# The order of r's weight tiles behind attention: tiles for both batches first

## The chip, the cores and the metric

The kernel runs on one core of one Trainium2 chip. The metric is device time of one execution in microseconds (us); lower is better. A core has a matrix engine (TensorE, PE in the rows, with its weight loads as PEld), VectorE (DVE), ScalarE (ACT), GpSimd (POOL) and SyncE (SP), which here issues the transfers (DMA) from memory.

## The reference

For two batches, causal attention over 12 heads (448 tokens, 64 channels a head) gives x (448 x 768 a batch). A token and channel mixer follows, then a gated block. Cut to its formulas:

```python
scores = np.where(mask, -1e9, q @ k.T / 8); attn = softmax(scores)
x = attn @ v                                  # (2, 448, 768)
h = np.maximum(x.T @ w_tok1, 0) @ w_tok2      # mixes tokens
u = x + h.T
r = np.maximum(u @ w_ch1, 0)                  # 768 -> 1536 channels
y = u + r @ w_ch2                             # 1536 -> 768 channels
uv = gelu(y @ w_in); a, b = halves of uv
out = y + (a * (w_sg @ layernorm(b) * g + b_sg)) @ w_out
```

The large weights come as float64 and are used with about float32 accuracy.

## The kernel before, in words

**Numbers.** Every operand of the large products is held as a pair of tiles, a high and a low part, and `mm3` (L132) makes three matmuls of each product: high by high, low by high, high by low.

**Weight tiles.** A weight tile of 128 x 768 numbers goes through one path (`load64`, L96, through `load_w`, L124). SyncE loads the raw float64 words (`wraw`, 768 KB, two buffers). ScalarE turns their upper halves into float32 (`wm`, L113, three buffers), VectorE shifts `wm` (L116) and adds bits of the lower halves (L117), ScalarE rounds `wm` to the high part (`whi`, L121, three buffers), and GpSimd subtracts it from `wm` for the low part (`wlo`, L94, three buffers). TensorE reads `whi` in a group's first matmul and `wlo` in its second or third.

**Stages.** Attention and the token mixer (L196 to L443) make u, batch 0 first and then batch 1, as `u_hi` and `u_lo`. Beside the second batch's attention, seven of the twelve tiles of r are made for batch 0 (`up`, L411; `NF0` is 7). Behind attention comes the **r stage** (L456): `channel_up` (L170) loads a tile of `w_ch1`, and for each batch that it is asked for makes a group of 18 matmuls (6 chunks by 3) into `r_ps`, and from it `rh` (ScalarE, L179) and `rl` (VectorE, L180). Tiles 0 to 6 are asked for batch 1 alone there, one group each, and tiles 7 to 11 for both batches, two groups each: 17 groups in all. Then the **y stage** (L458): for each of 6 output chunks, `channel_down` (L183) loads two halves of `w_ch2`, 768 KB each, and makes a group of 36 matmuls a batch, whose first 18 read the first half and the rest the second, in order of r's tiles; beside it a 512 KB tile of `w_in` is prepared as `wvh` and `wvl` (L460). The gated block follows.

**Order.** Each engine runs its instructions in the order in which a scheduler lists them; the scheduler goes by the program's order and a timeline of its own. An engine waits at an instruction until its operands and its output buffer are ready, and all behind it on that engine waits too.

Of the kernel before, what the change touches and what calls it, by code (L numbers as in the profile page):

```python
# [27 lines left out]
def mixer_kernel(  # L28
# [27 lines left out]
    NFF = 12  # L56
# [3 lines left out]
    NF0 = 7  # L60
# [35 lines left out]
    def load64(hi, lo, src, hi_eng="act", twice=False):  # L96


        n = src.shape[-1]
        raw = wpool.tile([P, WC], mybir.dt.int64, tag="wraw", name="wraw", bufs=2)[:, :n]  # L100
        if twice:
            nc.sync.dma_start(raw[:64], src)
            nc.sync.dma_start(raw[64:], src)
        else:
            nc.sync.dma_start(raw, src)
        words = raw.bitcast(I32).rearrange("p (n w) -> p n w", w=2)
        m = wpool.tile([P, WC], F32, tag="wm", name="wm", bufs=3)[:, :n]
        mi = m.bitcast(I32)

        nc.scalar.activation(  # L113
            m, words.bitcast(F32)[:, :, 1], AF.Prelu, scale=2.0 ** -112, alpha=-(2.0 ** 32)
        )
        nc.vector.tensor_scalar(mi, mi, 3, None, ALU.logical_shift_left)  # L116
        nc.vector.scalar_tensor_tensor(mi, words[:, :, 0], 29, mi, ALU.logical_shift_right, ALU.bitwise_or)  # L117
        if hi_eng == "pool":
            nc.gpsimd.tensor_scalar(hi, m, 1.0, 0.0, ALU.mult, ALU.add)
        else:  # L120
            nc.scalar.copy(hi, m)  # L121
        sub(lo, m, hi)
# [47 lines left out]
    def channel_up(m, batches, pool, psum):  # L170

        wh, wl = load_w(w_ch1[m])
        for b in batches:
            us = slice(b * S, (b + 1) * S)
            pr = psum.tile([P, 512], F32, tag="d", name="r_ps")
            mm3(pr[:, :S], [((wh[:, c, :], wl[:, c, :]), (u_hi[:, c, us], u_lo[:, c, us])) for c in range(NCC)])
            rh = pool.tile([P, S], F32R, tag=f"rh{m}_{b}", name="rh")
            rl = pool.tile([P, S], F32R, tag=f"rl{m}_{b}", name="rl")
            nc.scalar.activation(rh, pr[:, :S], AF.Relu)  # L179
            nc.vector.scalar_tensor_tensor(rl, pr[:, :S], 0.0, f32(rh), ALU.max, ALU.subtract)  # L180
            r_of[m, b] = (rh, rl)

    def channel_down(m, psum, tmp):  # L183

        ws = [load_w(w_ch2[m, :, c:c + NCC, :]) for c in (0, NCC)]
        for b in range(B):
            us = slice(b * S, (b + 1) * S)
            py = psum.tile([P, 512], F32, tag="d", name="y_ps")
            mm3(py[:, :S], [((ws[c // NCC][0][:, c % NCC, :], ws[c // NCC][1][:, c % NCC, :]), r_of[c, b]) for c in range(NFF)])
            t = tmp.tile([P, S], F32, tag="yt", name="yt")  # L190
            nc.vector.tensor_add(t, py[:, :S], f32(u_hi[:, m, us]))
            nc.vector.tensor_add(t, t, f32(u_lo[:, m, us]))
            nc.scalar.copy(u_hi[:, m, us], t)  # L193
            sub(u_lo[:, m, us], t, u_hi[:, m, us])
# [257 lines left out]
    with rs:  # L452
        ps_d = ctx.enter_context(tc.tile_pool(name="ps_d", bufs=8, space=PSUM, reuse_waits="tile"))
        r1pool = rs.enter_context(tc.tile_pool(name="r1pool", bufs=1, reuse_waits="tile"))
        tmp = rs.enter_context(tc.tile_pool(name="tmp", bufs=3, reuse_waits="tile"))
        for m in range(NFF):  # L456
            channel_up(m, [1] if m < NF0 else [0, 1], r1pool, ps_d)
        for m in range(NCC):  # L458
            channel_down(m, ps_d, tmp)
            load64(wvh[:, m, :], wvl[:, m, :], w_inv[:, m, :])  # L460
# [158 lines left out]
```

## Time and profile before

| | |
|---|---|
| time, median of 3 runs (lowest, highest) | 428.57 us (427.43, 428.97) |
| profiled execution: its own time | 429.13 us |
| profiled execution: its span, first to last instruction | 427.3 us |
| TensorE busy | 399.9 us, 94% of the span |
| mean granted TensorE clock, as a share of full speed | 0.988 |
| r stage (first group to first matmul of the y stage) | 169.02 to 231.12 us of the span |

The profiled execution is one run, 0.56 us above the median; 1.83 us of its time lie outside the span. Times in rows count from the span's start. Matmuls are pipelined, so one row lasts longer than the step from it to the next; the steps between starts tell TensorE's pace.

### The profile page before, as it was taken

The page shows a single profiled execution, that of the slowest core. Times are in us where ns is not written, and L with a number is a line of the kernel's source. Part 1 is how long each engine was busy: PE and PEld are TensorE (multiplying, and loading weights), DVE is VectorE, ACT ScalarE, POOL GpSimd, SP SyncE. Part 2 cuts the span into 40 slices and gives each one's busy share as a digit, 9 for nine tenths or more (in the row PEclk, how much of TensorE's full clock was granted, in tenths as well). Part 3 has the DMA queues.
Part 4 walks back from the last instruction along what each step waited for, and adds up shares of the span by engine and source line. Part 5 has one row for each costly group of instructions (what it writes and reads, how often), then busy time and mean ns, then how long its engine had stood idle before and what let it go on. Part 6 is the DMA issues. An engine that isn't in the chain of part 4 may idle for free.

```text
span 427.3 us, 6998 instructions
## 1 busy us (share of the span) xinstructions
PE 399.9 (94%) x2567; PEld 340.3 (80%) x2567; DVE 238.4 (56%) x522; ACT 204.2 (48%) x389; POOL 246.5 (58%) x234
## 2 busy tenths in 40 slices
PE   5878788888998999999999999999999999999996
PEld 3545666776787998999999999999998889965995
DVE  5989566787693645344444275557437451249422
ACT  3888678697665454445344244334423232332100
POOL 2789768769777564464335247454556653225662
PEclk9989999999898999999999999999999999999999
DMA  7999999999987854446344344453354001100122
GB/s 213 199 290 235 209 173 208 252 220 265 242 170 164 163 160 154 137 156 220 123 132 157 106 127 144 134 181 110 126 163 135 0 0 51 49 2 0 76 98 86
DMA packets 66738, 62.29 MB, mean 146 GB/s; under 512 B 53136, under 2 KB 58384, under 8 KB 66704
## 3 DMA queue, kind: packets, MB, share of 16 engines
q1 hardware_dynamic: 66704, 61.85, 56.5%
q8 instruction: 20, 0.33, 0.3%
q14 instruction: 14, 0.11, 0.1%
HBM read 46.50 MB, written 2.75 MB: 115 GB/s over the span
## 4 chain that ended last, share of the span: by engine, by line
PE 67%; DMA 12%; POOL 8%; ACT 5%; SPq 2%; issue 2%; DVE 2%; POOLq 0%; ACTq 0%; DVEq 0%
DMA pT<-hl 8%; PE y_ps L137 7%; PE y_ps L136 7%; PE y_ps L138 7%; PE r_ps L138 6%; PE r_ps L136 6%; PE r_ps L137 6%; POOL hl L301 4%; DMA vr<-in 2%; PE v_ps L138 2%; PE o_ps L136 2%; PE o_ps L138 2%; PE o_ps L137 2%; PE ug_ps L136 2%; PE v_ps L137 2%; PE ug_ps L138 2%
## 5 line engine op out<-in xcount | busy, mean ns | idle before, releaser
L94 POOL TENSOR_TENSOR wlo<-wm,whi 128x768 fp32r<-128x768 f32 (+1 forms) x41 | 81.3, 1984 | 75.6 <-ACT whi L121 75.1
L116 DVE TENSOR_SCALAR wm<-wm 128x768 int32<-128x768 int32 (+2 forms) x53 | 34.1, 643 | 88.0 <-ACT wm L113 88.0
L301 POOL TENSOR_TENSOR hl<-pe,hl 128x512 f16<-128x512 f32 x48 | 60.5, 1267 | 29.2 <-ACT hl L300 25.2
L113 ACT ACTIVATE wm<-wraw 128x768 f32<-128x768 f32 (+2 forms) x53 | 42.7, 805 | 59.1 <-POOL wlo L94 47.7
L286 PE MATMUL s_ps<-k,q 128*128 128x64 f32 (+3 forms) x216 | 57.9, 410 | 8.3 <-DMA q<-in 4.6
L138 PE MATMUL r_ps<-u_hi,wlo 128*128 128x448 f32 x144 | 53.4, 370 | 0.0
L137 PE MATMUL r_ps<-u_lo,whi 128*128 128x448 f32 x144 | 53.2, 369 | 0.0
L136 PE MATMUL r_ps<-u_hi,whi 128*128 128x448 f32 x144 | 53.1, 369 | 0.0
L136 PE MATMUL y_ps<-rh,whi 128*128 128x448 f32 x144 | 52.6, 365 | 0.0
L138 PE MATMUL y_ps<-rh,wlo 128*128 128x448 f32 x144 | 52.6, 365 | 0.0
L137 PE MATMUL y_ps<-rl,whi 128*128 128x448 f32 x144 | 52.6, 365 | 0.0
L121 ACT CAST whi<-wm 128x768 fp32r<-128x768 f32 (+1 forms) x41 | 32.8, 800 | 37.8 <-PE ug_ps L137 11.6
L117 DVE SCALAR_TENSOR_TENSOR wm<-wraw,wm 128x768 int32<-128x768 int32 (+2 forms) x53 | 50.1, 945 | 1.0
L286 PEld LDWEIGHTS s_ps<-k,q 128*128 128x128 f32 x216 | 32.4, 208 | 17.2 <-issue 6.6
L298 ACT ACTIVATE pe<-pe,bias 128x192 f32<-128x192 f32 (+3 forms) x84 | 40.2, 522 | 0.4
L291 DVE CUSTOM_DVE_ANT_0 pe<-s_ps,mask 128x320 f32<-128x320 f32 (+3 forms) x84 | 34.6, 444 | 7.9 <-PE s_ps L286 6.1
L300 ACT CAST hl<-pe 128x512 f16<-128x512 f32 x48 | 29.3, 612 | 18.3 <-DMA pT<-hl 17.9
L326 PE MATMUL x_ps<-vh,pT 128*128 128x65 f16 (+1 forms) x240 | 26.3, 197 | 11.6 <-DMA pT<-hl 10.9
L326 PEld LDWEIGHTS <-pT 128*128 128x128 f16 (+1 forms) x240 | 21.2, 98 | 19.6 <-DMA pT<-hl 14.6
L94 POOL TENSOR_TENSOR u_lo<-yt,u_hi 128x448 fp32r<-128x448 f32 x12 | 13.9, 1156 | 30.1 <-ACT u_hi L193 30.1
L138 PEld LDWEIGHTS r_ps<-u_hi,wlo 128*128 128x128 f32 x144 | 27.2, 189 | 2.6 <-issue 0.4
L136 PEld LDWEIGHTS r_ps<-u_hi,whi 128*128 128x128 f32 x144 | 27.3, 189 | 2.4 <-issue 0.2
(140 smaller groups left out, 918.7 us busy)
## 6 DMA issues: line engine op xcount, KB each, us to landing
wraw<-in SPq DMA_DIRECT2D x35, 768.0 KB, 4.5
wraw<-in SPq DMA_DIRECT2D x14, 512.0 KB, 3.9
vr<-in SPq DMA_DIRECT2D x12, 320.0 KB, 3.8
k<-in SPq DMA_DIRECT2D x12, 224.0 KB, 3.4
q<-in SPq DMA_DIRECT2D x24, 112.0 KB, 3.4
out<-ob SPq DMA_DIRECT2D x12, 224.0 KB, 1.9
wraw<-in SPq DMA_DIRECT2D x3, 256.0 KB, 3.1
pT<-hl SPq DMA_TRANSPOSE x48, 4.4
```

Source lines behind the costliest of these rows:

```text
L94: nc.gpsimd.tensor_sub(lo, src, f32(hi))
L113: nc.scalar.activation(m, words.bitcast(F32)[:, :, 1], AF.Prelu, scale=2.0 ** -112, alpha=-(2.0 ** 32))
L116: nc.vector.tensor_scalar(mi, mi, 3, None, ALU.logical_shift_left)
L117: nc.vector.scalar_tensor_tensor(mi, words[:, :, 0], 29, mi, ALU.logical_shift_right, ALU.bitwise_or)
L136: nc.tensor.matmul(ps, lh, rh, start=i == 0 and not begun, stop=False)
L137: nc.tensor.matmul(ps, lh, rl, start=False, stop=False)
L138: nc.tensor.matmul(ps, ll, rh, start=False, stop=i == n - 1)
L286: nc.tensor.matmul(ps[:, o:o + m], qp[:, q0:q0 + P], k2[:, ks], start=True, stop=True)
L291: nc.vector.tensor_tensor_reduce(out=pe[:, cs], in0=ps[:, cs], in1=mask0 if i == 0 else mask[:, MASKS[i]], scale=-1.0 / math.sqrt(D), scal ...
L298: nc.scalar.activation(pe[:, cs], pe[:, cs], AF.Exp, bias=bias[:, j:j + 1], scale=-1.0)
L301: nc.gpsimd.tensor_sub(hl[:, 1], pe, hl[:, 0])
L326: nc.tensor.matmul(o, ph, vh[:, c, h, :D + 1], start=j == 0, stop=False)
```

## The change

The loop of the r stage lists the tiles in another order: tiles 7 to 11, each for both batches, come first, and tiles 0 to 6, for batch 1 alone, behind them. Nothing else is edited; the same loads, matmuls and evictions are made.

```diff
-        for m in range(NFF):
+        for m in [*range(NF0, NFF), *range(NF0)]:
             channel_up(m, [1] if m < NF0 else [0, 1], r1pool, ps_d)
         for m in range(NCC):
             channel_down(m, ps_d, tmp)
```

On TensorE and on SyncE the rows, read without buffer numbers, stand in the same order before and after; which tile a row works on differs. On GpSimd the order differs where the r stage meets the y stage. The rows below begin with the last low parts of x that attention makes; `wlo` rows are weight tiles, `wvl` those of `w_in`.

```order
 L94 TENSOR_TENSOR xl<-xf,xh 128x3x128
 L94 TENSOR_TENSOR xh<-xf,xh 64x64 x2
-L94 TENSOR_TENSOR wlo<-wm,whi 128x768 x11
+L94 TENSOR_TENSOR wlo<-wm,whi 128x768 x12
 L94 TENSOR_TENSOR wvl<-wm,wvh 128x512
 L94 TENSOR_TENSOR wlo<-wm,whi 128x768 x2
 L94 TENSOR_TENSOR wvl<-wm,wvh 128x512
-L94 TENSOR_TENSOR wlo<-wm,whi 128x768
 L94 TENSOR_TENSOR u_lo<-yt,u_hi 128x448
 L94 TENSOR_TENSOR wlo<-wm,whi 128x768 x2
```

Eleven `wlo` are the remaining tiles of r; in the changed kernel the first half of `w_ch2` comes as the twelfth, ahead of the first `wvl`, where it stood behind it.

On ScalarE, the rows of the kernel before where the last two tiles of r (for both batches) give way to `w_ch2`: `wm_3187` and `wm_3299` belong to `w_in`, `wm_3197` and `wm_3207` to the second chunk's halves of `w_ch2`, `whi_3081` and `whi_3091` are the first chunk's two halves, and the `rh` are of tiles 9 to 11.

```order
L113 ACTIVATE wm_3187<-wraw_3185 128x512
L179 ACTIVATE rh_2942<-r_ps_2923 128x448
L121 CAST wvh_2559<-wm_3187 128x512
L113 ACTIVATE wm_3197<-wraw_3195 128x768
L121 CAST whi_3081<-wm_3085 128x768
L179 ACTIVATE rh_2965<-r_ps_2946 128x448
L113 ACTIVATE wm_3207<-wraw_3205 128x768
L179 ACTIVATE rh_2998<-r_ps_2979 128x448
L121 CAST whi_3091<-wm_3095 128x768
L179 ACTIVATE rh_3021<-r_ps_3002 128x448
L113 ACTIVATE wm_3299<-wraw_3297 128x512
L179 ACTIVATE rh_3054<-r_ps_3035 128x448
```

And at the same place of the changed kernel, where the last tiles are those for one batch: `whi_3048` is tile 6, the last of r, and the `rh` are of tiles 3 to 5.

```order
L113 ACTIVATE wm_3095<-wraw_3093 128x768
L121 CAST whi_3048<-wm_3052 128x768
L179 ACTIVATE rh_2978<-r_ps_2959 128x448
L113 ACTIVATE wm_3187<-wraw_3185 128x512
L121 CAST whi_3081<-wm_3085 128x768
L179 ACTIVATE rh_3011<-r_ps_2992 128x448
L121 CAST wvh_2559<-wm_3187 128x512
L113 ACTIVATE wm_3197<-wraw_3195 128x768
L121 CAST whi_3091<-wm_3095 128x768
L179 ACTIVATE rh_3044<-r_ps_3025 128x448
L113 ACTIVATE wm_3207<-wraw_3205 128x768
L121 CAST whi_3193<-wm_3197 128x768
```

Between two `whi` there was one eviction `rh` or two before; now there is one, and `whi_3081` stands ahead of `wvh_2559`, where it stood behind it.

## Rows read from the trace of the kernel before

**Rows 1.** Stretches of the span: busy us (instructions) of each engine, granted clock, DMA.

```profile
core 0: us, PE busy (x) PEld busy (x) DVE busy (x) ACT busy (x) POOL busy (x), PEclk, DMA share, GB/s
0.00:133.00 133.00, 110.44 (x1047) 83.93 (x1047) 97.75 (x309) 97.44 (x224) 98.75 (x123) 0.97 1.02 221
133.00:169.00 36.00, 34.71 (x279) 31.65 (x280) 18.23 (x32) 19.62 (x35) 22.88 (x22) 0.95 0.63 166
169.00:231.10 62.10, 62.10 (x309) 57.58 (x308) 27.65 (x43) 28.22 (x43) 27.51 (x13) 1.00 0.47 151
231.10:338.00 106.90, 106.90 (x516) 96.73 (x516) 59.09 (x78) 37.79 (x53) 58.11 (x42) 1.00 0.41 128
338.00:427.30 89.30, 85.78 (x421) 70.45 (x420) 35.64 (x61) 21.10 (x36) 39.22 (x36) 1.00 0.12 43
```

**Rows 2.** Waits of TensorE from 165 us to the end: total, times, longest.

```profile
PE u_ps L377 <- ACT ah L366: 0.7, 1, 0.7
```

**Rows 3.** TensorE in order of time: start, us, operation; start and end of stages.

```profile
165.56 0.47 PE L377 MATMUL u_ps<-w2h,ah 128*128 128x448 f32 x1 [0.69 <-ACT ah L366]
...
169.02 0.45 PE L136 MATMUL r_ps<-u_hi,whi 128*128 128x448 f32 x1
169.30 0.36 PE L137 MATMUL r_ps<-u_lo,whi 128*128 128x448 f32 x1
169.50 0.36 PE L138 MATMUL r_ps<-u_hi,wlo 128*128 128x448 f32 x1
...
231.12 0.36 PE L136 MATMUL y_ps<-rh,whi 128*128 128x448 f32 x1
...
423.41 0.37 PE L138 MATMUL o_ps<-gt_hi,wlo 128*128 128x448 f32 x1
```

**Rows 4.** GpSimd in order of time: low parts of r's tiles 3 to 9.

```profile
173.66 1.85 POOL L94 TENSOR_TENSOR wlo<-wm,whi 128x768 fp32r<-128x768 f32 x1 [6.57 <-ACT whi L121]
177.36 2.36 POOL L94 TENSOR_TENSOR wlo<-wm,whi 128x768 fp32r<-128x768 f32 x1 [1.86 <-ACT whi L121]
181.51 2.43 POOL L94 TENSOR_TENSOR wlo<-wm,whi 128x768 fp32r<-128x768 f32 x1 [1.79 <-ACT whi L121]
185.74 2.44 POOL L94 TENSOR_TENSOR wlo<-wm,whi 128x768 fp32r<-128x768 f32 x1 [1.79 <-ACT whi L121]
189.97 2.44 POOL L94 TENSOR_TENSOR wlo<-wm,whi 128x768 fp32r<-128x768 f32 x1 [1.79 <-ACT whi L121]
...
198.42 2.43 POOL L94 TENSOR_TENSOR wlo<-wm,whi 128x768 fp32r<-128x768 f32 x1 [1.79 <-ACT whi L121]
203.06 2.42 POOL L94 TENSOR_TENSOR wlo<-wm,whi 128x768 fp32r<-128x768 f32 x1 [2.21 <-ACT whi L121]
```

**Rows 5.** ScalarE in order of time: two tiles of the r stage.

```profile
172.75 0.83 ACT L121 CAST whi<-wm 128x768 fp32r<-128x768 f32 x1 [2.91 <-PE r_ps L137]
...
179.75 0.90 ACT L113 ACTIVATE wm<-wraw 128x768 f32<-128x768 f32 x1 [2.08 <-POOL wlo L94]
180.56 0.82 ACT L121 CAST whi<-wm 128x768 fp32r<-128x768 f32 x1
181.28 0.54 ACT L179 ACTIVATE rh<-r_ps 128x448 fp32r<-128x448 f32 x1
```

**Rows 6.** VectorE in order of time: the passes of one tile of the r stage.

```profile
180.69 0.56 DVE L116 TENSOR_SCALAR wm<-wm 128x768 int32<-128x768 int32 x1 [2.14 <-ACT wm L113]
181.28 0.96 DVE L117 SCALAR_TENSOR_TENSOR wm<-wraw,wm 128x768 int32<-128x768 int32 x1
182.16 0.62 DVE L180 SCALAR_TENSOR_TENSOR rl<-r_ps,rh 128x448 fp32r<-128x448 f32 x1
```

**Rows 7.** The raw weight tiles' loads from 165 to 231 us: issue to landing.

```profile
DMA to landing us min/median/max: 3.8/4.2/4.7
```

**Rows 8.** GpSimd, then ScalarE, in order of time: a tile of `w_in` between two weight tiles.

```profile
210.19 1.84 POOL L94 TENSOR_TENSOR wlo<-wm,whi 128x768 fp32r<-128x768 f32 x1 [4.71 <-ACT whi L121]
214.65 1.28 POOL L94 TENSOR_TENSOR wvl<-wm,wvh 128x512 fp32r<-128x512 f32 x1 [2.62 <-ACT wvh L121]
217.71 2.44 POOL L94 TENSOR_TENSOR wlo<-wm,whi 128x768 fp32r<-128x768 f32 x1 [1.78 <-ACT whi L121]
...
212.06 0.66 ACT L113 ACTIVATE wm<-wraw 128x512 f32<-128x512 f32 x1 [1.56 <-POOL wlo L94]
```

**Rows 9.** Stretches around TensorE's last long wait in attention; columns as in the first group.

```profile
131.50:133.60 2.10, 0.26 (x6) 0.13 (x4) 0.00 (x0) 2.10 (x6) 1.47 (x2) 1.00 1.06 202
133.60:137.00 3.40, 3.40 (x16) 3.15 (x17) 0.62 (x1) 3.09 (x7) 3.37 (x3) 0.51 0.86 251
```

## The prediction

> **What bounds the kernel now.** I read the stretches first. From 169 to 338 us TensorE is busy in every microsecond, 62.10 of 62.10 us in the r stage and 106.90 of 106.90 us in the y stage, at a granted clock of 1.00, while no other engine is busy for more than 59 us of the second of them [rows 1]. Busy matmuls can hide small holes, so I then read the list of TensorE's waits: from 165 us to the end there is one, of 0.7 us, ahead of the last token mix, for ScalarE [rows 2]. The starts in order of time confirm it: the r stage's 17 groups run from 169.02 to 231.12 us [rows 3], so a group of 18 matmuls takes 62.10 / 17 = 3.65 us and a matmul 0.203 us, and the last matmul of the kernel starts at 423.41 us, some 4 us ahead of the span's end. Behind attention the kernel is as long as its matmuls. A reordering takes none of them away. It can gain only a wait that is there, 0.7 us, and it can lose by making TensorE wait.
>
> **Who could make it wait.** A tile for one batch keeps TensorE for 3.65 us, a tile for two for 7.31 us. Against this stands the path that prepares a tile. Its pace is read from the low parts on GpSimd: they end at 175.51, 179.72, 183.94, 188.18 and 192.41 us, 4.22 us apart [rows 4]. Rows of one tile show why: `wlo` ends at 179.72, the next `wm` starts at 179.75, `whi` follows at 180.56 on the same engine, and the next `wlo` starts at 181.51 [rows 4, 5]. So for a tile for one batch the path is 4.22 - 3.65 = 0.57 us too slow, and TensorE lives on a lead. With three buffers of `whi`, the lead is largest when a tile follows work that gave the path time: tile 3's `whi` waits for the end of tile 0's group (169.02 + 3.65 = 172.67) and starts at 172.75; its `wlo` ends at 175.51, that is 2.84 us behind the buffer's release [rows 4, 5]. Its group starts at 179.98 and reads `wlo` in its second or third matmul, by 180.18 on the early count: a lead of 4.67 us. From there before's leads are 4.11, 3.55, 2.96 and 2.38 us for tiles 4 to 7, and then the tiles for two batches restore it. That is why no wait is recorded.
>
> **The change part by part.**
>
> *The start of the r stage.* Tile 7's first group needs only batch 0's u, made long before. It could have been put into the 0.7 us wait, but the row order on TensorE is the one of before: the group follows the last token mix. The first group of before did not wait for u either [rows 3]. Gain: 0; at the most 0.7 us if the row order did not tell it.
>
> *Five tiles for both batches first.* Ten groups, 169.02 to 205.55 us. The path has 7.31 us for each 4.22 us of work; even with two `rh` between (203.06 + 2.42 = 205.48 against 198.42 + 2.43 = 200.85, 4.63 us [rows 4]) it keeps up. Cost 0.
>
> *Seven tiles for one batch behind them.* Their groups start at 205.55, 209.20, 212.86, 216.51, 220.16, 223.82 and 227.47 us. Tiles 0 and 1 have free buffers earlier. Tile 2 takes the buffer that tile 11 frees at 205.55; by the row of tile 3 before, its `wlo` ends 2.84 us later, at 208.39, for 213.06: a lead of 4.67 us, as before. Then 0.57 us is lost a tile: tiles 3 to 6 end at 212.61, 216.83, 221.05 and 225.27 us, for 216.71, 220.36, 224.02 and 227.67; leads 4.10, 3.53, 2.97 and 2.40 us. Cost 0.
>
> *What now follows them.* Before, tiles for two batches stood here and gave time back. Now the y stage does: its first group reads the first half of `w_ch2` in its first 18 matmuls (231.12 us) and the second half from 234.77 us, two more loads at one per 3.65 us. The first half is ready at 225.27 + 4.22 = 229.49 for 231.32: lead 1.83 us. The second half shares the path with a tile of `w_in`. The nearest rows are before's own such place: from the end of a `wlo` at 212.03, through `wm` of `w_in` at 212.06 and `wvl`, to the end of the next `wlo` at 217.71 + 2.44 = 220.15, 8.12 us [rows 8]. In the new order on ScalarE `wm_3187` stands ahead of `whi_3081`, so I count the 8.12 us from tile 6's `wlo` (225.27), which gives 233.39 for 234.97: lead 1.58 us. Counted from the first half's `wlo` (229.49) it would be 237.61, a wait of 2.64 us; I take the first, since the work on `w_in` then overlaps the first half's `wlo`, and keep the other for the range. Behind it the first group's partner of 36 matmuls gives 7.31 us back with no new half needed. Cost 0.
>
> *Evictions.* `rh` of tile 6 now stands behind `whi_3193` on ScalarE, which waits for tile 6's buffer, freed at 231.12. Its `rl` is done some 6 us later at the worst; the first reader is batch 1's group, matmul 19 on, at 238.43 + 3.65 = 242.08 us. Cost 0.
>
> *Loads.* SyncE may load two tiles ahead. A load takes 3.8 to 4.7 us [rows 7], and at 4.22 us a tile a `wraw` buffer comes round every 8.44 us, of which `wm` to the end of L117 holds it for 2.49 us (179.75 to 182.24 [rows 5, 6]); 2.49 + 4.7 = 7.2 us fits. Seven tiles in a row at this pace ran before without a wait for a load.
>
> **Sum.** 0 + 0 + 0: the span stays 427.3 us and that execution 429.13 us. The median shown is 0.56 us lower, so I predict **428.6 us**.
>
> **A rule against the sum.** A low part takes 1.85 us where VectorE runs no L117, and 2.43 us where it starts during one (181.51, inside 181.28 to 182.24) [rows 4, 6]: 0.58 us more. The Trainium skill (SBUF — State Buffer, section Who interferes with whom) calls the ports that VectorE and GpSimd share an exclusive lock that an instruction holds to its end, and says that a VectorE instruction with two SBUF inputs contends with a GpSimd instruction that reads SBUF. The trace agrees, since 0.58 us is about what is left of L117. By the rule the pace is thus a matter of who starts first. Rows tell what the bad case would be: if both of VectorE's passes (0.56 + 0.96 us [rows 6]) held each `wlo`, it would last 3.37 us instead of 2.43 and the pace would be 5.16 us; that is the second rival.
>
> **The rivals.**
>
> 1. *The second half of `w_ch2` is late (slower).* If the tile of `w_in` is not overlapped, TensorE waits 2.64 us at 234.77 us. The only comparable hole, 2.10 us with 0.26 us of work, was followed by 3.40 us at a granted clock of 0.51, the lower level of 1.2 GHz, though before it the clock was full [rows 9]; that costs another 1.7 us. 428.6 + 4.3 = 432.9 us. It decides from a delay of 1.58 us on. Against it speaks the row order.
> 2. *The path's pace is 5.16 us (slower).* From 208.39 us, tile 6 ends at 229.03, 1.36 us late, and the first half at 234.19, 2.87 us late in all; with the clock 1.7 us more: 433.2 us. Against it: six low parts in a row at 4.22 us, with VectorE's passes in the order that the new kernel keeps.
> 3. *The wait of 0.7 us goes (faster, barely).* 427.9 us. The order speaks against it, and it would not be told from no change. A gain above 2.1 us has no place behind 165 us, and nothing ahead of it is moved.
>
> **How the numbers follow.** A measurement tells this kernel's change from none at about 0.5%, 2.1 us. No wait added or removed: 0.87. Rival 1: 0.05. Rival 2: 0.03. Rival 3: 0.04, within 0.5% too. I leave 0.01 for a gain that I do not see. So faster 0.02, same 0.90, slower 0.08. The runs shown spread from 427.43 to 428.97, 1.1 us below and 0.4 us above their median; with rival 3 below, and above a part of rival 1's wait without the clock's fall (up to about 1.5 us), the range is 427.1 to 430.1 us, and it leaves out the two slower rivals.
>
> **What would show it.** In the changed kernel's profile TensorE's waits behind 165 us should still hold one row, of 0.7 us for ScalarE, and the y stage should start at about 231.1 us. Low parts of tiles 2 to 6 and of the first half of `w_ch2` should end about 4.22 us apart between 208 and 230 us, and the second half's before 234.8 us. Wrong would be a wait for `wlo` or `whi` between 216 and 240 us, a pace above 4.6 us, or a granted clock below 1.00 in the r or y stage.

## The result and the profile after

The changed kernel took 432.82 us in the median of 14 runs (428.20 to 434.67), the kernel before 427.26 us in 14 runs beside it (424.49 to 428.97). The run of 434.67 us counts as a slow one and is left out of the ratio, which is 1.0119, 95% interval 1.0092 to 1.0145: the change made the kernel slower by about 5.1 us (3.9 to 6.2), and the time lies above the predicted range.

The profiled execution of the changed kernel has a time of 430.92 us and a span of 429.1 us. Its stretches are the r stage, the y stage and the rest; columns as in [rows 1].

```profile
166.80:228.90 62.10, 62.10 (x310) 57.55 (x309) 24.85 (x38) 26.03 (x39) 22.73 (x12) 1.00 0.39 125
228.90:320.50 91.60, 88.90 (x433) 80.82 (x432) 53.14 (x61) 32.85 (x47) 44.14 (x29) 1.00 0.44 144
320.50:429.10 108.60, 105.10 (x504) 86.02 (x502) 48.38 (x84) 27.24 (x45) 55.04 (x51) 1.00 0.17 56
```

The y stage of the kernel before in the same view, to the first matmul of the gated block:

```profile
231.10:318.70 87.60, 87.60 (x434) 81.18 (x434) 46.39 (x56) 32.20 (x46) 44.34 (x28) 1.00 0.43 134
```

The r stage, the only one whose order was edited, takes 62.10 us in both. What follows the y stage takes 108.6 us in both. The y stage went from 87.55 us (231.12 to 318.67) to 91.60 us, TensorE's clock at 1.00 throughout: 4.05 us, within the interval of the loss. The r stage begins 2.2 us earlier here than in [rows 3]. Nothing ahead of it was edited, and further profiles of kernels that differ only behind it have it between 164 and 169 us, so I compare lengths of stages and not the two spans.

The list of TensorE's waits from 163 us to the end shows what came in beside the one wait of [rows 2]:

```profile
PE y_ps L138 <- POOL wlo L94: 2.7, 4, 0.9
PE u_ps L377 <- ACT ah L366: 0.7, 1, 0.7
```

TensorE in order of time, at the first of the four. The other three follow at 278.44, 294.11 and 309.86 us, one in each chunk of the y stage from the third on, each time at the first `wlo` of the chunk's second half of `w_ch2`.

```profile
261.93 0.37 PE L137 MATMUL y_ps<-rl,whi 128*128 128x448 f32 x1
262.87 0.47 PE L138 MATMUL y_ps<-rh,wlo 128*128 128x448 f32 x1 [0.57 <-POOL wlo L94]
263.18 0.36 PE L136 MATMUL y_ps<-rh,whi 128*128 128x448 f32 x1
```

Two steps of 0.94 + 0.31 us stand there in place of 2 x 0.20: 0.85 us lost. The four places lose 0.85, 0.99, 0.80 and 1.17, together 3.8 of the 4.05 us.

GpSimd of the changed kernel in order of time. The first four rows are single tiles of r (4 to 6) and the first half of `w_ch2`, the answer to [rows 4]; the next two are the `w_in` tile and, in one row, two halves of `w_ch2` (the second for chunk 1, the first for chunk 2); then come the second half for chunk 2, the first for chunk 3 and the second for chunk 3.

```profile
212.16 2.44 POOL L94 TENSOR_TENSOR wlo<-wm,whi 128x768 fp32r<-128x768 f32 x1 [1.77 <-ACT whi L121]
216.38 2.44 POOL L94 TENSOR_TENSOR wlo<-wm,whi 128x768 fp32r<-128x768 f32 x1 [1.78 <-ACT whi L121]
220.61 2.44 POOL L94 TENSOR_TENSOR wlo<-wm,whi 128x768 fp32r<-128x768 f32 x1 [1.79 <-ACT whi L121]
224.60 2.04 POOL L94 TENSOR_TENSOR wlo<-wm,whi 128x768 fp32r<-128x768 f32 x1 [1.56 <-ACT whi L121]
226.60 1.28 POOL L94 TENSOR_TENSOR wvl<-wm,wvh 128x512 fp32r<-128x512 f32 x1
228.43 4.71 POOL L94 TENSOR_TENSOR wlo<-wm,whi 128x768 fp32r<-128x768 f32 x2 [0.55 <-POOL wvl L94]
...
245.31 1.85 POOL L94 TENSOR_TENSOR wlo<-wm,whi 128x768 fp32r<-128x768 f32 x1
248.72 1.85 POOL L94 TENSOR_TENSOR wlo<-wm,whi 128x768 fp32r<-128x768 f32 x1 [1.56 <-issue]
...
260.97 1.84 POOL L94 TENSOR_TENSOR wlo<-wm,whi 128x768 fp32r<-128x768 f32 x1
```

The second halves' low parts start at 245.31, 260.97, 276.56, 292.24 and 307.99 us, 15.6 to 15.8 us a chunk, where TensorE needs 4 x 3.65 = 14.60. Before they started at 243.02, 257.62, 272.21, 286.80 and 301.39 us, 14.59 us apart.

VectorE of the changed kernel, at the entry of the y stage and then a whole chunk of it. The rows of 128x512 are the `w_in` tile.

```profile
230.15 1.29 DVE L116 TENSOR_SCALAR wm<-wm 128x768 int32<-128x768 int32 x1 [0.31 <-ACT wm L113]
231.47 2.48 DVE L117 SCALAR_TENSOR_TENSOR wm<-wraw,wm 128x768 int32<-128x768 int32 x1
...
247.90 0.43 DVE L116 TENSOR_SCALAR wm<-wm 128x512 int32<-128x512 int32 x1 [3.56 <-ACT wm L113]
248.24 0.62 DVE L191 TENSOR_TENSOR yt<-y_ps,u_hi 128x448 f32<-128x448 f32 x1
248.77 2.35 DVE L117 SCALAR_TENSOR_TENSOR wm<-wraw,wm 128x512 int32<-128x512 int32 x1
...
256.44 0.56 DVE L116 TENSOR_SCALAR wm<-wm 128x768 int32<-128x768 int32 x1 [0.97 <-ACT wm L113]
257.04 0.96 DVE L117 SCALAR_TENSOR_TENSOR wm<-wraw,wm 128x768 int32<-128x768 int32 x1
257.91 0.62 DVE L191 TENSOR_TENSOR yt<-y_ps,u_hi 128x448 f32<-128x448 f32 x1
258.56 0.62 DVE L192 TENSOR_TENSOR yt<-yt,u_lo 128x448 f32<-128x448 f32 x1
263.54 0.43 DVE L116 TENSOR_SCALAR wm<-wm 128x512 int32<-128x512 int32 x1 [4.35 <-ACT wm L113]
...
264.41 2.35 DVE L117 SCALAR_TENSOR_TENSOR wm<-wraw,wm 128x512 int32<-128x512 int32 x1
```

ScalarE of the changed kernel in the same chunk, with the two waits for a load ahead of it in the first rows:

```profile
238.43 0.90 ACT L113 ACTIVATE wm<-wraw 128x768 f32<-128x768 f32 x1 [2.22 <-DMA wraw<-in]
241.45 0.89 ACT L113 ACTIVATE wm<-wraw 128x768 f32<-128x768 f32 x1 [2.13 <-DMA wraw<-in]
...
243.97 0.83 ACT L121 CAST whi<-wm 128x768 fp32r<-128x768 f32 x1
247.19 0.67 ACT L113 ACTIVATE wm<-wraw 128x512 f32<-128x512 f32 x1 [2.39 <-POOL wlo L94]
247.77 0.83 ACT L121 CAST whi<-wm 128x768 fp32r<-128x768 f32 x1
...
255.52 0.89 ACT L113 ACTIVATE wm<-wraw 128x768 f32<-128x768 f32 x1 [2.46 <-DMA wraw<-in]
259.22 0.57 ACT L193 CAST u_hi<-yt 128x448 fp32r<-128x448 f32 x1 [2.81 <-DVE yt L192]
259.69 0.83 ACT L121 CAST whi<-wm 128x768 fp32r<-128x768 f32 x1
262.85 0.66 ACT L113 ACTIVATE wm<-wraw 128x512 f32<-128x512 f32 x1 [2.32 <-POOL wlo L94]
```

And the same chunk of the kernel before: VectorE, then one row of GpSimd, then two of ScalarE:

```profile
245.60 0.43 DVE L116 TENSOR_SCALAR wm<-wm 128x512 int32<-128x512 int32 x1 [5.71 <-ACT wm L113]
245.94 0.62 DVE L191 TENSOR_TENSOR yt<-y_ps,u_hi 128x448 f32<-128x448 f32 x1
246.48 0.68 DVE L117 SCALAR_TENSOR_TENSOR wm<-wraw,wm 128x512 int32<-128x512 int32 x1
247.08 2.28 DVE L192 TENSOR_TENSOR yt<-yt,u_lo 128x448 f32<-128x448 f32 x1
...
246.67 2.20 POOL L94 TENSOR_TENSOR wlo<-wm,whi 128x768 fp32r<-128x768 f32 x1 [1.81 <-ACT whi L121]
...
244.89 0.67 ACT L113 ACTIVATE wm<-wraw 128x512 f32<-128x512 f32 x1 [2.01 <-POOL wlo L94]
245.70 0.83 ACT L121 CAST whi<-wm 128x768 fp32r<-128x768 f32 x1
```

Here is the difference. Before, L117 on the `w_in` tile starts at 246.48 us, 0.19 us ahead of GpSimd's `wlo`, and takes 0.68 us. After, it starts at 248.77 us, 0.05 us behind the `wlo` at 248.72, and takes 2.35 us: to the end of that `wlo` and its own 0.6 us more. The two starts have moved against each other by 0.24 us, and 1.67 us hang on it. VectorE is held up by this `wlo` before, too, but there it is L192, one instruction later, that takes 2.28 us, and L192 holds no raw buffer.

The 0.24 us come from `whi` on ScalarE. Before, `whi` starts 0.81 us behind the `wm` of the `w_in` tile (244.89, 245.70): it waits for its buffer, which TensorE gives back at the end of chunk 1, at 231.12 + 14.6 = 245.7 us. After, that buffer is free at 228.90 + 14.6 = 243.5 us, `whi` follows `wm` by 0.58 us (247.19, 247.77), and `wlo` starts about 0.23 us earlier against L117, which follows the same `wm` by 1.58 to 1.59 us in both. So with these passes L117 is ahead only while ScalarE waits for TensorE: `whi` follows by 0.79 to 0.81 us in every such chunk of the kernel before, and by 0.56 to 0.57 us in the chunks of e2, e3, e4 and e7 below, in all of which L117 is behind. No run changed this wait alone.

The 1.67 us stand in a loop, because L117 is the last reader of a `wraw` buffer. In the chunk above: L117 2.35 us; the next load into the freed buffer, to `wm`'s start at 255.52, 4.40; `wm` to L116 0.92, to L117 0.60, to L191 0.87, to L192 0.65, to `u_hi` 0.66, to `whi` 0.47, to `wlo` (260.97) 1.28, to `wm` of the next `w_in` tile 1.88, to its L116 0.69, to L191 0.34, to its L117 (264.41) 0.53. Together 15.64 us, the pace that is seen. With 0.68 in place of 2.35 the loop would be 13.97 us, shorter than TensorE's 14.60.

### The profile page after: what moved, and what is told of

It reads as the page before. It is cut to its first block, busy times and chain, and to the rows that moved or that the text cites. A ratio compares the mean times of both kernels' runs of the same rounds, so it can differ in the third digit from the quotient of the medians.

```text
span 429.1 us, 7000 instructions
## 1 busy us (share of the span) xinstructions
PE 400.2 (93%) x2567; PEld 338.6 (79%) x2567; DVE 242.3 (56%) x522; ACT 203.3 (47%) x389; POOL 243.9 (57%) x234
## 5 line engine op out<-in xcount | busy, mean ns | idle before, releaser
L94 POOL TENSOR_TENSOR wlo<-wm,whi 128x768 fp32r<-128x768 f32 (+1 forms) x41 | 77.1, 1882 | 79.3 <-ACT whi L121 70.7
L116 DVE TENSOR_SCALAR wm<-wm 128x768 int32<-128x768 int32 (+2 forms) x53 | 33.0, 623 | 87.1 <-ACT wm L113 87.1
L301 POOL TENSOR_TENSOR hl<-pe,hl 128x512 f16<-128x512 f32 x48 | 61.8, 1295 | 27.2 <-ACT hl L300 24.2
L117 DVE SCALAR_TENSOR_TENSOR wm<-wraw,wm 128x768 int32<-128x768 int32 (+2 forms) x53 | 63.2, 1193 | 0.9
L94 POOL TENSOR_TENSOR u_lo<-yt,u_hi 128x448 fp32r<-128x448 f32 x12 | 15.8, 1320 | 31.2 <-ACT u_hi L193 31.2
L138 PEld LDWEIGHTS y_ps<-rh,wlo 128*128 128x128 f32 x144 | 27.0, 188 | 6.4 <-POOL wlo L94 4.2
L180 DVE SCALAR_TENSOR_TENSOR rl<-r_ps,rh 128x448 fp32r<-128x448 f32 x24 | 14.9, 621 | 25.7 <-ACT rh L179 25.4
```

Of the source, the lines that this page charges most:

```text
L94: nc.gpsimd.tensor_sub(lo, src, f32(hi))
L138: nc.tensor.matmul(ps, ll, rh, start=False, stop=i == n - 1)
L301: nc.gpsimd.tensor_sub(hl[:, 1], pe, hl[:, 0])
```

## The experiments

Theories A, B and C in the first expectations: A, L117's lost start makes the slow rhythm of 15.64 us a chunk; B, the late raw loads alone pace the y stage, whoever starts first; C, the path's work for a chunk is longer than TensorE's 14.6 us, so a lost lead never comes back. Theory D, in the later ones, is A with the raw buffer in the loop and the loss graded by the lead at the entry. All ratios are to the kernel before on the same chip. Every kernel was timed in five rounds, 6 to 12 runs each. The diffs are cut to the lines that matter; the parameters that lead to them are left out.

**e1, another second pass on the `w_in` tile**, with one tile as input. It leaves the upper words of these tiles out.

```diff
-        nc.vector.scalar_tensor_tensor(mi, words[:, :, 0], 29, mi, ALU.logical_shift_right, ALU.bitwise_or)
+        nc.vector.tensor_scalar(mi, words[:, :, 0], 29, None, ALU.logical_shift_right)   # w_in tiles only
```

> The changed kernel, in which the last VectorE pass on each tile of w_in (L117, 128x512) shifts the raw words into wm and no longer reads wm too: one input from SBUF instead of two. It leaves the upper words of w_in's v half out of the result; every engine's order stays that of the changed kernel. Theory A (the y stage falls into a slow rhythm of about 15.64 us a chunk because this pass starts 0.05 us behind a low part on GpSimd and waits for it, 2.35 us instead of 0.68): the pass takes about 0.7 us, the chunk 14.6 us, TensorE waits for no wlo, the y stage takes about 87.5 us as before instead of 91.6, and the time is 427 to 428 us. Theory B (the late raw loads alone pace the y stage: two buffers, 4.4 us a load, whoever holds which port): the y stage stays near 91 us and the time near 432 us. Theory C (the lead lost by seven tiles for one batch in a row is simply never won back, since a chunk needs more of the path than 14.6 us): as B.

Measured: 430.89 us, ratio 1.0088 (1.0057 to 1.0119), y stage 91.06 us, four waits of 1.8 us in all. VectorE at the entry and in a chunk:

```profile
233.69 0.43 DVE L117 TENSOR_SCALAR wm<-wraw 128x512 int32<-128x512 int32 x1
...
248.09 2.08 DVE L117 TENSOR_SCALAR wm<-wraw 128x512 int32<-128x512 int32 x1
```

The premise fell: the pass with one input takes 0.43 us alone, but 2.08 us when it starts 0.05 us behind a `wlo` (248.04). The experiment thus took nothing away and tells no theory apart, except that it is not L117's second input that makes it wait.

**e2, a raw buffer of their own for the `w_in` tiles.**

```diff
+        raw = rp.tile([P, 512], mybir.dt.int64, tag="wvraw", name="wvraw", bufs=1)   # w_in tiles only
-            load64(wvh[:, m, :], wvl[:, m, :], w_inv[:, m, :])
+            load64(wvh[:, m, :], wvl[:, m, :], w_inv[:, m, :], rp=wvp)
```

> The changed kernel with a raw buffer of its own (4 KB a partition) for the tiles of w_in, so that a late L117 on such a tile holds up no load of w_ch2. Theory A and theory B both have the loop of the slow rhythm run from that L117 through the next raw load (about 4.4 us), so both expect it to be cut: no wait for wlo, y stage about 87.5 us, time 427 to 428 us. Theory C: the path's work is the same, so the y stage stays near 91 us and the time near 432 us.

Measured: 428.40 us, ratio 1.0017 (0.9985 to 1.0049), y stage 87.56 us, no wait for `wlo`. VectorE in a chunk:

```profile
244.66 2.34 DVE L117 SCALAR_TENSOR_TENSOR wm<-wvraw,wm 128x512 int32<-128x512 int32 x1
```

L117 still loses 1.66 us, and the second halves come 14.6 to 14.8 us apart all the same, since no weight tile's load waits for this buffer. So the long L117 costs only through the buffer that it holds, and the path's work alone is not too long: C falls.

**e3 and e4, the order again**: the last double tile behind the singles (7 to 10, 0 to 6, 11), and only four singles behind (0 to 2, 7 to 11, 3 to 6).

```diff
-        for m in [*range(NF0, NFF), *range(NF0)]:
+        for m in [*range(NF0, NFF - 1), *range(NF0), NFF - 1]:          # e3
+        for m in [*range(NF0 - 4), *range(NF0, NFF), *range(NF0 - 4, NF0)]:   # e4
```

> The changed kernel with tile 11, for both batches, put behind the seven tiles for one batch (order 7 to 10, 0 to 6, 11). Theory A: the 7.31 us of the last tile give the path 3.1 us of lead back, the y stage is entered with whi waiting for TensorE and stays at 14.6 us a chunk: y stage about 87.5 us, time 427 to 428 us. If what costs time is the row of seven tiles for one batch itself (as the second rival of the prediction had it), the time stays at about 432 us.

> Order 0 to 2, 7 to 11, 3 to 6: four tiles for one batch at the end instead of seven. Theory A: the cost is one of two rhythms, not a price per tile. At the y stage's entry the lead is 4 x 0.57 = 2.3 us smaller than behind a tile for both batches, against 4.0 us with seven; the time is either about 427.5 us or about 432, with the y stage at 87.5 or 91.6 us, and not in the middle. Theory C (a lead that is lost per tile and not won back): in the middle, about 4/7 of the loss, 430 us.

Measured: e3 427.73 us, ratio 0.9997 (0.9966 to 1.0028), y stage 88.23 us, one wait of 0.4 us; e4 429.05 us, 1.0024 (0.9994 to 1.0053), 88.10 us, one wait of 0.3 us. In both L117 on the `w_in` tile takes 2.3 us and the rhythm is 15.6 us a chunk, as in the changed kernel. The times are near those that theory A gave, but not for its reason: it had the rhythm at 14.6 us in e3, and one of two rhythms, with all of the loss or none, in e4. The rhythm alone does not make the loss, then: these two entered the y stage with more in hand and had used it up only in the last chunk.

**e5, the competitor taken away**: in the y stage VectorE itself subtracts the low parts of the first halves.

```diff
+        if lo_eng == "dve":                      # first halves of w_ch2
+            nc.vector.tensor_sub(lo, m, f32(hi))
```

> The changed order; in the y stage VectorE, not GpSimd, subtracts the lower parts of the first halves of w_ch2 (768 words), and its queue has this directly behind L117 on the w_in tile. So GpSimd has nothing to hold the port with while L117 reads the w_in tile's raw buffer. Theory D (L117 loses the port to GpSimd's wlo, 2.35 for 0.68 us, which turns a loop of 14.0 us into one of 15.6, over the 14.6 of TensorE): L117 takes about 0.7, the second halves' lower parts start about 14.6 us apart, the y stage takes 87.5 to 88.5 us, time 427 to 429. Rival L (the loop of raw load, wm, two passes, the additions and the two casts is over 14.6 us with or without the port): 15.3 to 15.7 us a chunk, y stage 91 to 92, time 431.5 to 433.

Measured: 426.77 us, ratio 0.9987 (0.9956 to 1.0019), y stage 87.56 us, no wait for `wlo`. VectorE in a chunk, where L123 is the subtraction moved here:

```profile
257.15 0.68 DVE L117 SCALAR_TENSOR_TENSOR wm<-wraw,wm 128x512 int32<-128x512 int32 x1
257.75 0.95 DVE L123 TENSOR_TENSOR wlo<-wm,whi 128x768 fp32r<-128x768 f32 x1
```

L117 is back at 0.68 us, with the shared raw buffers, and the second halves start 13.8 to 14.6 us apart. Rival L falls, and theory B with it.

**e6, e2's buffer in the kernel before.**

> The kernel before, with a raw buffer of its own for the w_in tiles, as in e2. Control for e2. Theory D: the kernel before is paced by TensorE at 14.6 us a chunk already, so the buffer is worth nothing: ratio 0.998 to 1.002, y stage 87.3 to 87.8. Rival G (the buffer is a gain of its own that hid a loss of the change elsewhere, so e2 said nothing about the cause): ratio about 0.990, y stage about 84.

Measured: 427.22 us, ratio 1.0004 (0.9977 to 1.0031), y stage 87.56 us. The buffer is worth nothing where L117 wins; e2 removed the loss and did not cover it.

**e7, six singles behind the doubles.**

```diff
+        for m in [0, *range(NF0, NFF), *range(1, NF0)]:
```

> The changed order with one single tile (0) ahead of the double tiles, six behind them. Leads of the second half of w_ch2 at the entry of the y stage so far: 4.7 us (before, all singles ahead), 3.6 (four singles behind, e4), 0.2 (seven behind). Theory D: the lead at the entry is between, about 1.3 us by a straight line from four to seven, the rhythm is 15.6 us a chunk, and what the lead doesn't pay of the four times 1.04 us is lost: about 2.9 us (1.5 to 3.8), time 429.5 to 431. Rival N (an all-or-nothing loss that comes with the seventh single tile alone): nothing is lost, 427.7; and if any fifth single tile already brings all of it, 432 to 433.

Measured: 432.35 us, ratio 1.0117 (1.0070 to 1.0164), y stage 91.75 us, four waits of 2.8 us in all. The straight line between four and seven singles was wrong: six already bring all of it. The lead at the entry was 0.4 us and not 1.3.

**e8, the same work with an earlier second pass.**

```diff
+            nc.vector.tensor_scalar(words[:, :, 0], words[:, :, 0], 29, None, ALU.logical_shift_right)   # 512 words
+            nc.vector.scalar_tensor_tensor(mi, mi, 3, words[:, :, 0], ALU.logical_shift_left, ALU.bitwise_or)
```

> The changed order; for tiles of 512 words VectorE's two passes share the work in another way: the first shifts the low words of the raw buffer in place, which needs no wm from ScalarE, the second shifts wm and joins the two. Same number of passes, same engines, same buffers. In VectorE's queue the second pass now stands ahead of the addition L191 (in the changed kernel L191 stands between the passes), and so starts some 0.9 us earlier, ahead of GpSimd's wlo of the first half instead of 0.05 us behind it. Theory D: the second pass takes about 0.7 us, wlo starts after it, the second halves' lower parts are 14.6 us apart, TensorE's waits for wlo go, y stage 87.5 to 88.5 us, time 427 to 428.5. Rival L' (it was the shift of the subtraction's work from GpSimd in e5, or the buffer in e2, that gave the time, not who starts first): second pass about 2.3 us, 15.6 us a chunk, time 431 to 433.

Measured: 428.51 us, ratio 1.0042 (1.0015 to 1.0068), y stage 87.67 us, no wait for `wlo`. VectorE and GpSimd in a chunk:

```profile
249.59 0.69 DVE L118 SCALAR_TENSOR_TENSOR wm<-wm,wraw 128x512 int32<-128x512 int32 x1 [2.44 <-ACT wm L113]
...
250.41 1.85 POOL L94 TENSOR_TENSOR wlo<-wm,whi 128x768 fp32r<-128x768 f32 x1 [1.55 <-issue]
```

The second pass (L118 here) is first by 0.8 us and takes 0.69 us; the second halves start 14.05 us apart, near the 13.97 worked out above. This kernel entered the y stage with no lead at all and lost nothing in it: a late entry alone is harmless too. The 1.8 us (0.0042 x 427.23) by which it is slower than the kernel before lie ahead of the r stage, since that stage takes 62.10 us here and what follows the y stage 108.6 us, as before. The edit also touches two tiles of `w_tok2` beside attention (and six of `w_out` behind the y stage), which no run took apart; the wait ahead of the last token mix is 1.3 us here, where it was 0.7.

**e9, the kernel before with a later L117.**

```diff
-        nc.vector.tensor_scalar(mi, mi, 3, None, ALU.logical_shift_left)
+        for k in ((2, 1) if n == 512 else (3,)):
+            nc.vector.tensor_scalar(mi, mi, k, None, ALU.logical_shift_left)
```

> The kernel before, in its own order, with the shift by 3 of tiles of 512 words made in two passes, by 2 and by 1. That is 0.43 us more for VectorE a tile, and in its queue both additions (L191, L192) now stand ahead of L117, so that in the y stage L117 on the w_in tile starts about 1 us later, behind GpSimd's wlo instead of 0.19 us ahead of it. Theory D: L117 takes over 2 us, the raw buffer comes free some 2.5 us later, and the kernel before falls into the slow rhythm too: 15.6 to 16.6 us a chunk; with its lead of 4.7 us at the entry that costs 0 to 4 us, so 427.5 to 432. Rival S (only the order of the r stage's tiles, by the late entry, makes the slow rhythm; VectorE is busy for under 60 of 107 us and has room for 0.43 us a chunk): 14.6 us a chunk, no wait, ratio 0.998 to 1.002.

Measured: 436.56 us, ratio 1.0215 (1.0172 to 1.0259), y stage 92.08 us. VectorE in a chunk, with GpSimd's `wlo` as the last row, and TensorE's waits from 172 us on:

```profile
265.39 2.07 DVE L117 TENSOR_SCALAR wm<-wm 128x512 int32<-128x512 int32 x1
...
267.92 0.68 DVE L118 SCALAR_TENSOR_TENSOR wm<-wraw,wm 128x512 int32<-128x512 int32 x1
...
265.34 1.84 POOL L94 TENSOR_TENSOR wlo<-wm,whi 128x768 fp32r<-128x768 f32 x1 [1.55 <-ACT whi L122]
```

```profile
PE y_ps L139 <- POOL wlo L94: 1.6, 1, 1.6
PE y_ps L137 <- ACT whi L122: 0.7, 1, 0.7
```

The order of r's tiles is that of before, the lead at the entry is the 4.7 us of before, and yet the y stage loses 4.5 us: the added shift starts 0.05 us behind a `wlo`, from the tile's first pass to the end of L118 it takes 4.09 us (264.51 to 268.60), where it took 1.56 before (245.60 to 247.16), and the chunks are 16.2 to 16.3 us apart until the lead is gone. Rival S falls. Behind the wait of 1.6 us the granted clock was 0.53 over 313.5 to 317 us, the lower level of 1.2 GHz, and nine matmuls follow each other there by 0.37 to 0.44 us in place of 0.20: about 1.6 of the 4.5 us. The time is beyond the 427.5 to 432 us that were expected: the rest of the 9.3 us by which e9 is slower lies ahead of the r stage, which starts at 171.59 us; there two tiles of `w_tok2` have the added shift as well.

**e10, e8's passes in every tile.**

> The changed order with the passes of e8 in every tile. Theory D: the path of a tile loses the first pass (0.56 us) between wm and whi, in the r stage too, so single tiles follow each other at about 3.7 us instead of 4.22 and the lead at the y stage's entry stays above 3 us; with the second pass ahead of wlo the rhythm stays at 14.6: time 426.5 to 428.5, as before, not better, since TensorE has its matmuls. Rival: the in-place pass on the raw words, 128x768 with a stride, now holds the port against GpSimd at other places and the pace gets worse: 430 to 434.

Measured: 434.48 us, ratio 1.0177 (1.0136 to 1.0218). Single tiles follow each other at 3.65 us as expected and L117 on the `w_in` tile takes 0.69 us, but the time is worse. The r stage starts only at 172.54 us, so most of the loss lies ahead of it; and the y stage takes 88.92 us. VectorE there:

```profile
266.10 0.96 DVE L116 TENSOR_SCALAR wraw<-wraw 128x768 int32<-128x768 int32 x1 [3.09 <-DMA wraw<-in]
267.41 0.69 DVE L117 SCALAR_TENSOR_TENSOR wm<-wm,wraw 128x512 int32<-128x512 int32 x1 [0.35 <-ACT wm L113]
```

The rival was half right: a new wait, but not for a port. The first pass of the next tile now stands at the head of VectorE's queue and waits 3.09 us for its load, with the `w_in` tile's second pass behind it.

No version beats the kernel before by more than its interval.

## Why the prediction was wrong

**Right.** The r stage costs nothing: 62.10 us, single tiles 4.2 us apart (212.16, 216.38, 220.61), no wait. The start of the stage, its evictions and the wait of 0.7 us are as foreseen. So is the entry: the first half of `w_ch2` was counted ready 1.83 us ahead of its reader and ended at 226.64 for 229.10, a lead of 2.46. The second was counted at 1.58; `wlo` of that half, the first of the two in the row of 228.43, ends at 231.02 for 232.75, a lead of 1.73. Neither slower rival happened: not the wait that rival 1 named, not the pace of 5.16 us, and the clock stayed at 1.00. That rival 1's figure, 432.9 us, lies next to the measured 432.82 is luck. None of the prediction's three signs of being wrong came either (a wait between 216 and 240 us, a pace above 4.6 us, a clock below 1.00): the waits begin at 262.87 us. What told was the list of waits, which was to hold one row and holds two. The forecast also started 1.3 us too high, since the three runs that it knew had a median of 428.57 us and the 14 runs have 427.26.

**The step that failed** is the end of "What now follows them": "Behind it the first group's partner of 36 matmuls gives 7.31 us back with no new half needed. Cost 0." The count stopped at chunk 1. I took the y stage as a place with time to spare because TensorE never waited there before, and did not work out the path's own pace there, three loads and three pairs of passes for each 14.60 us. At the entry two `wlo` back to back stretch VectorE's passes to 1.29 and 2.48 us (230.15, 231.47), ScalarE then waits 2.22 and 2.13 us for loads, and chunk 2's second half gets its `whi` at 243.97, 15.07 us into the stage; before it came at 242.05, 10.93 us in, as soon as its buffer was free. The lead there fell from 4.7 to 0.2 us, and from then on each chunk loses another 1.04.

**The rule was weighed at the wrong place.** I asked of the Trainium skill (SBUF — State Buffer, section Who interferes with whom) what the exclusive lock does to `wlo`, and only in the r stage. The same section says that issue order, not op shape, decides who blocks; the rows agree, with 0.68 against 2.35 us for one instruction. What had to be asked was which of VectorE's instructions a `wlo` could hold up, and what hangs on that one's end.

**What the runs put in its place.** Two numbers make the loss: the lead with which chunk 2's second half comes (the end of its `wlo` against 18.45 us after the stage's start, the early count of the prediction), and the pace of the second halves over chunks 2 to 6. TensorE should lose what the halves fall behind 14.60 us a chunk, less the lead, at the worst chunk:

| kernel | lead, us | pace, us a chunk | loss by this rule, us | y stage less 87.55, us |
|---|---|---|---|---|
| before | 4.7 | 14.59 | 0 | 0 |
| after | 0.2 | 15.67 | 4.1 | 4.05 |
| e1 | -0.1 | 15.39 | 3.3 | 3.5 |
| e2 own buffer | 2.6 | 14.69 | 0 | 0.0 |
| e3 double last | 3.4 | 15.63 | 0.7 | 0.7 |
| e4 four behind | 3.6 | 15.65 | 0.6 | 0.55 |
| e5 `wlo` on VectorE | 3.2 | 14.2 | 0 | 0.0 |
| e6 before, own buffer | 4.7 | 14.59 | 0 | 0.0 |
| e7 six behind | 0.4 | 15.74 | 4.2 | 4.2 |
| e8 second pass early | -0.2 | 14.05 | 0.2 | 0.1 |
| e9 before, later L117 | 4.7 | 16.53 | 3.0 | 4.5 |
| e10 all tiles | 1.95 | 15.12 | 1.4 | 1.4 |

Only e9 is off, by 1.5 us, about the 1.6 us that the fallen clock costs. The causes of the pace are shown: e5 takes the subtraction away from GpSimd, e8 gives VectorE the first start, and in both the pace returns; e2 lets VectorE lose and cuts the buffer out of the loop; e9 makes the kernel before lose it. That two things must come together, a lead used up and a lost first start, is shown by e3 and e4 (slow, with lead, nearly free) and e8 (no lead, fast, free).

Open: the kernel is 5.1 us slower and the profiled y stage only 4.05; the interval (3.9 to 6.2) allows both, and no run tells whether a microsecond more lies elsewhere. The profiled execution, at 430.92 us, is among the faster of its kernel. Nor did I take apart why six singles behind the doubles use up the lead and four do not; the long passes at the entry are seen in the rows at 230.15 and 231.47, but no run changed them alone.

## What to carry to other kernels

A stage in which the bound engine never waits may still have a path with only some tenths of a microsecond to spare, and that path must be timed as a loop, buffer by buffer, before it is counted on to give time back. Where two engines can hold each other up, as VectorE and GpSimd do here (0.68 against 2.35 us), look for the pairs of instructions that start within some tenths of each other and ask what the loser holds; a buffer in a loop made a shift of 0.24 us into a loss of 1 us that returned every round. A loss shows where the lead runs out, here 34 us and two chunks behind the edited stage, so the place of the wait is not the place of the cause.

## What was not expected of the hardware

A shift with one input and a stride over the raw words, 0.43 us alone, takes 2.08 us when it starts 0.05 us behind GpSimd's subtraction (e1), and a shift on contiguous words 2.07 us (e9). The pass with two inputs takes 2.35 there. All three end behind the subtraction, the shifts by 0.3 us and the pass by 0.6. The Trainium skill (SBUF — State Buffer, section Who interferes with whom) lists `tensor_scalar` among the operations that can take the shared pair; the rows agree.
